# Attention and routed experts on one core: V gathers alone on SyncE's DMA queue, every other attention load and store on ScalarE's

## Chip, cores, metric
One NeuronCore of a Trainium2 chip runs the whole program in one launch. The metric is device time in microseconds (us), the median of several executions. A profiled execution gives the trace; all times inside the kernel below are counted from the start of its span.

## What is computed
Block-sparse attention (4 sequences, 8 heads, 768 tokens, head size 64, blocks of 32 tokens) and then a cosine router that sends each of the 3072 tokens to one of 8 experts (512 -> 1024 -> 512, ReLU), all in float32:

```python
mask = |blk_i - blk_j| <= 1, or either block is the first or the last, or blk_j in sampled_blocks[blk_i]
attn = softmax(where(mask, q @ k.T / 8, -1e9))          # per head
x = (attn @ v), heads side by side                      # (3072, 512)
idx = argmax(normalize(x) @ normalize(expert_emb).T);  gate = softmax(logits / tau)[idx]
out = gate * (relu(x @ w1[idx]) @ w2[idx])
```

## The kernel before
**Stages.** Attention runs in 24 steps `s` (and one closing step), six per sequence: `b, c = divmod(s, 6)`. A step handles a chunk of 128 query rows. The chunks are shifted by one block: chunk c = 0 of a sequence holds the two end blocks (first and last), whose rows attend to every key, and two inner blocks; the other chunks hold four inner blocks. Then come 25 expert tiles of 128 tokens (two of them mixed from two experts), which are bound by TensorE.

**Order.** In attention each engine runs its instructions in the order in which the Python code issues them; nothing is reordered. So does each of the two queues that issue plain DMAs: SyncE's (SP) and ScalarE's (ACT). A DMA issue stands in its engine's instruction stream, and an instruction that waits holds up everything behind it on that engine. The order of a step `s` on TensorE (PE) is: `score_near(s)` (scores against near and end blocks, tile `ac`), `score_far(s)` (against the three sampled blocks of each query block, tile `dps`), `weigh_near(s-1, 0)`, at c = 0 `score_ends` (`bps`, four head pairs), `turn_x(s-2)`, at c = 1 to 4 `turn_k` (transposes one head pair of the next sequence's K, tile `kps`), `weigh_far(s-1)` (probabilities times gathered V; at c = 1 also the end rows' part), `turn_q(s+1)` (transposes the next chunk's Q), `chunk_logits(s-2)`, `weigh_near(s-1, 1)`, `normalize(s-1)`. `ac`, `dps`, `bps` and `kps` take turns on two PSUM buffers (`big`), so every one of them waits until ScalarE or VectorE has read the one before last: the exponentials `pac` (of `ac`), `pd` (of `dps`) and `pb` (of `bps`), and the copy `kt` (of `kps`). `normalize` ends with a Square on ScalarE (tile `sq`), which stands on ScalarE just ahead of the next step's `pac`.

**Loads.** `load_q(s+2)` fetches a chunk of Q (256 KB, two buffers), `load_k` a head pair of K in two DMAs of 192 KB (two buffers), `load_v` the next sequence's V in ten DMAs (`vst`, `vg0`), `gather_v` the sampled V blocks: 12 DMAs of 64 KB a step (6 at c = 0), one for each query block and sampled slot, with three buffers `vg` in turn. Their addresses come from a table `offset` in SBUF, which the issuing engine reads into registers once for each c (`shifts`) and keeps. `gather_k` copies the sampled K blocks inside SBUF (GpSimd and VectorE), `near_v` near V blocks (GpSimd). `route` (line 771) stores each finished sequence's x rows to DRAM for the experts' gathers. Slots 0 and 1 of `gather_v`, all of `load_q` after the first two, `load_k`, most of `load_v`, the x stores and the expert weights (line 1060) are issued by SP; slot 2 of `gather_v` by ACT, in the middle of the step behind `pd`. SP's program at the start of step s is: `load_k`, `load_q(s+2)`, `gather_v(s+1)` slots 0 and 1, `load_v`.

**Start.** `load_block_ids`, four K pairs and two Q chunks, V of the first sequence, warm-up matmuls, constants, `build_choice` (the offset table and the bias that masks sampled blocks already covered), four `turn_k`, `turn_q(0)`, `gather_k(0)`, `gather_v(0)`, and the loop.

Of the kernel before, what the change touches and what calls it, by code (L numbers as in the profile page):

```python
# [20 lines left out]
P = 128  # L21
# [2 lines left out]
NB = S // BLK  # L24
NRAND = 3
NC = S // P
NPAIR = H // 2
N = B * S
NT = B * NC
# [100 lines left out]
def build_tokens(k, shifted):  # L130

    nc, pool = k.nc, k.const
    tok = pool.tile([P, NT], I32, name="tok")
    nc.gpsimd.iota(tok, pattern=[[-S, B], [-P, NC]], base=N + BLK * shifted, channel_multiplier=-1)
    if shifted:
        first = tok.rearrange("p (b c) -> p b c", c=NC)[:, :, 0]
        for rows, by in ((slice(0, BLK), -BLK), (slice(BLK, D), D - BLK - S)):
            nc.vector.tensor_scalar(out=first[rows], in0=first[rows], scalar1=by, scalar2=None, op0=ALU.add)
# [177 lines left out]
def pieces(c, shifted=True):  # L316

    if not shifted:
        return [(slice(0, P), c * P)]
    if c:  # L320
        return [(slice(0, P), c * P - BLK)]
    return [(slice(0, BLK), 0), (slice(BLK, D), S - BLK), (slice(D, P), BLK)]


def load_block_ids(k):
# [7 lines left out]
def build_choice(k):  # L333

    nc, pool = k.nc, k.setup
    r = pool.tile([P, NRAND, NI], F32, name="rand")
    nc.vector.tensor_copy(out=r, in_=k.idb[:, 1:NB - 1, :, 0].rearrange("p n r -> p r n"))
    at = pool.tile([P, NRAND, NI], F32, name="at_block")
    nc.vector.tensor_scalar(out=at, in0=r, scalar1=0.0, scalar2=float(NB - 1), op0=ALU.max, op1=ALU.min)
    k.offset = k.const.tile([P, NRAND, NI], I32, name="offset")  # L340
    nc.vector.tensor_scalar(out=k.offset, in0=at, scalar1=float(BLK), scalar2=None, op0=ALU.mult)
    own = pool.tile([P, NI], F32, name="own_block")
    nc.gpsimd.iota(own, pattern=[[1, NI]], base=1, channel_multiplier=0, allow_small_or_imprecise_dtypes=True)
    bad = pool.tile([P, NRAND, NI], F32, name="bad_block")
# [16 lines left out]
    k.shift = {}  # L361


def shifts(k, engine, s, c):

    blocks = [NG * c + g - 2 for g in blocks_of(c)]
    key = engine, s, c
    if key not in k.shift:
        _, values = k.nc.values_load_multi_w_load_instructions(
            k.offset[0:1, s, blocks[0]:blocks[-1] + 1], engines=(engine,), min_val=0, max_val=S - BLK,  # L370
            skip_runtime_bounds_check_because="the block numbers are clamped to the blocks there are")
        k.shift[key] = list(values)
    return k.shift[key]


def load_q(k, n, engine=None):

    b, c = divmod(n, NC)
    k.raw["q", n] = t = k.ld.tile([P, H, D], F32, name="qraw", tag="qraw", bufs=2)
    src = k.q[b].rearrange("h s d -> s h d")  # L380
    for rows, lo in pieces(c):
        (engine or k.nc.sync).dma_start(out=t[rows], in_=src[lo:lo + rows.stop - rows.start])


def load_k(k, g, pool=None):

    b, j = divmod(g, NPAIR)
    k.raw["k", g] = t = (pool or k.ld).tile([P, NC, 2, D], F32, name="kraw", tag="kraw", bufs=2)
    for h in range(2):
        k.nc.sync.dma_start(out=t[:, :, h], in_=k.k[b, 2 * j + h].rearrange("(c p) d -> p c d", p=P))  # L390


def load_v(k, b):
# [22 lines left out]
    return slice(lo, lo + BLK), tile // 2  # L416


def gather_v(k, n, slots):

    b, c = divmod(n, NC)
    k.vg[n] = t = k.vg_ring[n % len(k.vg_ring)]
    src = k.v[b].rearrange("h s d -> s h d")
    for s in slots:
        lanes = slice(s * BLK, (s + 1) * BLK)
        engine, queue = ((mybir.EngineType.SP, k.nc.sync) if s < 2 else (mybir.EngineType.Activation, k.nc.scalar))
        for g, shift in zip(blocks_of(c), shifts(k, engine, s, c)):
            queue.dma_start(out=t[lanes, g, :, 0:D], in_=src[bass.ds(shift, BLK)])


def near_v(k, n):
# [9 lines left out]
def turn_k(k, g):  # L441

    nc = k.nc
    b, j = divmod(g, NPAIR)
    raw = k.raw.pop(("k", g))
    ps = k.big.tile([P, 2, 512], F32, name="kps", tag="big")
    for c in range(NC):
        nc.tensor.transpose(ps[:, c // 3, c % 3 * P:(c % 3 + 1) * P], raw[:, c].rearrange("p h d -> p (h d)"), k.ident)  # L448
    copy = nc.scalar.copy if g % 2 else nc.vector.tensor_copy
    copy(out=k.kt[b % 2][:, j].rearrange("p (w t) -> p w t", w=2), in_=ps[:, :, 0:3 * P])  # L450
    if j == NPAIR - 1:
        nc.scalar.copy(out=k.ke[b % 2].rearrange("p j (n t) -> p j n t", n=2),
                       in_=k.kt[b % 2].rearrange("p j (n t) -> p j n t", t=BLK)[:, :, 0:NB:NB - 1])


def turn_q(k, n):
# [268 lines left out]
def route(k, b):  # L725
# [40 lines left out]
    with ExitStack() if k.attending else k.tc.issue_after(picked):  # L766
        nc.vector.reciprocal(out=x[:, :, :, P], in_=gate.broadcast_to([P, NC, ND]))
    yield
    for c in range(NC):
        for rows, lo in pieces(c, not k.exact):  # L770
            nc.sync.dma_start(out=k.x_dram[b * S + lo:b * S + lo + rows.stop - rows.start, :],
                              in_=x[rows, c].rearrange("p e w -> p (e w)"))
        yield

# [418 lines left out]
def attention_fast(n, ctx):  # L1193
# [27 lines left out]
    warm_up(n, 10)  # L1221
    for i in range(2):
        nc.gpsimd.memset(n.vst[i][:, :, :, D:D + 1], 1.0)
        nc.gpsimd.memset(n.vg0[i][D:P, :, D:D + 1], 1.0)
        nc.gpsimd.memset(n.qt_ring[i], 0.0)
    for vg in n.vg_ring:
        nc.gpsimd.memset(vg, 0.0)
# [13 lines left out]
    for s in range(NCH + 1):  # L1241
# [6 lines left out]
                if (when, part) == (s, half):  # L1248
                    what()

        if s == 0:
            for g in range(NPAIR, NPAIR + 2):
                load_k(n, g)
        if 2 <= c and b + 1 < B:
            g = NPAIR * (b + 1) + c
            if g < B * NPAIR:
                load_k(n, g)
        if s + 2 < NCH:
            load_q(n, s + 2)
        if s + 1 < NCH:  # L1260
            gather_v(n, s + 1, (0, 1))
        if 1 <= c <= NPAIR and b + 1 < B:
            for to, src in load_v(n, b + 1)[3 * c - 3:3 * c]:
                nc.sync.dma_start(out=to, in_=src)
        if s < NCH:
            score_near(n, s)
            score_far(n, s)
# [17 lines left out]
        if s >= 1:  # L1285
            weigh_far(n, s - 1)
        if s + 1 < NCH:
            gather_v(n, s + 1, (2,))
            near_v(n, s + 1)
            turn_q(n, s + 1)  # L1290
        if s >= 2:
# [236 lines left out]
```

## Time and profile before

| | |
|---|---|
| median of 3 runs | 687.17 us (683.32 to 691.76) |
| the profiled execution | 691.73 us, of which the span is 690.0 us |
| mean granted TensorE clock | 0.939 of full |
| busy: PE, PE weight loads, VectorE, ScalarE, GpSimd | 612.8, 479.5, 220.2, 120.6, 238.8 us |
| first score matmul of step 0 | 19.52 us |
| first matmul of the first expert tile | 312.76 us |
| SP's queue (q1) and ACT's queue (q10), bytes | 149.32 MB and 7.08 MB |

A row of the list of waits is: engine, line and tile that waited, whose end released it, us in total, times, longest. A row of the timeline is: start, length, engine (a `q` behind it means its instruction queue, where DMAs are issued), line, operation, out <- in, shapes, count; in brackets the idle time ahead and what ended it. A row of the chain is: start, length, what; it follows the end of the program back through whatever released each piece. The row of windows gives busy time (and count) of each engine, the granted clock, the share of time that the 16 DMA engines were busy, and GB/s.

### The profile page before, as it was taken

How to read it: one execution, taken by the hardware profiler on the slowest of the kernel's cores; microseconds unless marked ns; L12 is line 12 of the kernel's file. 1: busy time of each engine (PE TensorE's matmuls, PEld its weight loads, DVE VectorE, ACT ScalarE, POOL GpSimd, SP SyncE). 2: the span in 40 equal slices, each digit the busy share in tenths (PEclk: the TensorE clock that was granted, in tenths of full speed). 3: DMA queues.
4: the chain of work that ended last, by engine and by line, in shares of the span. 5: the costliest groups of instructions: out<-in, count | busy, mean ns of one | idle time of the engine just before them, and what ended most of it. 6: DMA issues, size and time to landing. Idle time of an engine off the chain costs nothing.

```text
span 690.0 us, 21717 instructions
## 1 busy us (share of the span) xinstructions
PE 612.8 (89%) x9016; PEld 479.5 (69%) x9016; DVE 220.2 (32%) x659; ACT 120.6 (17%) x274; POOL 238.8 (35%) x447
## 2 busy tenths in 40 slices
PE   5896679796979699578999999999999999999996
PEld 3795679686878689577677667766477664776673
DVE  4563225342354366323571111121211212112110
ACT  1532233243242253221000000000000000000000
POOL 5662314432442253500202224432244223442232
PEclk7899779897998799979899999999999999999999
DMA  9846645577557854789999999999899998999811
GB/s 189 162 100 145 138 108 122 124 149 170 148 114 156 173 137 107 193 190 301 394 368 402 376 356 322 336 339 345 313 361 409 392 406 320 372 410 392 317 47 31
DMA packets 192318, 171.32 MB, mean 248 GB/s; under 512 B 152712, under 2 KB 152840, under 8 KB 189394
## 3 DMA queue, kind: packets, MB, share of 16 engines
q1 hardware_dynamic: 157794, 149.32, 67.9%
q0 software_dynamic: 5216, 13.43, 5.4%
q10 hardware_dynamic: 29200, 7.08, 5.1%
q8 instruction: 73, 1.20, 0.7%
q14 instruction: 35, 0.29, 0.1%
HBM read 157.17 MB, written 12.90 MB: 246 GB/s over the span
## 4 chain that ended last, share of the span: by engine, by line
PE 82%; DMA 9%; SPq 3%; DVE 2%; issue 2%; ACT 1%; DVEq 0%; POOL 0%; ACTq 0%; POOLq 0%
PE hp L1107 24%; PE yp L1122 23%; PE av L572 10%; PE dps L537 6%; DMA qraw<-in_q_dram 3%; PE yp L679 3%; DMA vg<-in_v_dram 3%; PE ac L513 3%; PE xg_ps L461 2%; DMA kraw<-in_k_dram 2%; PE hp L1150 2%; PE yp L1170 2%; PE bps L559 2%; PE kps L448 2%; PE xg_ps L668 1%
## 5 line engine op out<-in xcount | busy, mean ns | idle before, releaser
L1107 PEld LDWEIGHTS hp<-xgt,w 128*128 128x128 f32 x1472 | 167.6, 192 | 10.2 <-issue 10.2
L1107 PE MATMUL hp<-xgt,w 128*128 128x128 f32 x1472 | 168.4, 275 | 0.0
L1122 PE MATMUL yp<-w,h 128*128 128x512 f32 x368 | 163.7, 598 | 0.0
L1122 PEld LDWEIGHTS yp<-w,h 128*128 128x128 f32 x368 | 69.0, 193 | 78.2 <-issue 77.5
L1031 POOL DMA_INDIRECT xg<-x_dram,quarter x88 | 88.5, 1006 | 30.1 <-issue 27.4
L478 POOL COPY kg<-kt 128x128 f32 x176 | 45.2, 299 | 101.6 <-issue 79.6
L1131 POOL DMA_INDIRECT out_dram<-y,slot_l x20 | 20.2, 1011 | 156.8 <-DVE y L1130 156.8
L1110 ACT ACTIVATE h<-hp 128x512 f32<-128x512 f32 x23 | 13.7, 597 | 294.0 <-PE hp L1107 267.2
L1114 DVE TENSOR_SCALAR h<-hp 128x512 f32<-128x512 f32 x23 | 15.9, 691 | 154.0 <-PE hp L1107 154.0
L465 DVE COPY qt<-xg_ps 64x512 f32<-64x512 f32 x48 | 33.1, 689 | 89.4 <-PE xg_ps L461 88.6
L438 POOL COPY vg<-vst 32x520 f32<-32x520 f32 x80 | 49.4, 617 | 34.1 <-PE av L572 24.7
L572 PE MATMUL av<-vst,pac 64*64 64x65 f32 x1056 | 49.3, 233 | 2.1 <-issue 1.4
L537 PE MATMUL dps<-qt,kg 128*64 128x64 f32 x1408 | 49.7, 230 | 0.9 <-issue 0.6
L537 PEld LDWEIGHTS dps<-qt,kg 128*64 128x64 f32 x1408 | 45.8, 143 | 3.2 <-issue 0.7
L461 PE MATMUL xg_ps<-ident,qraw 128*128 128x128 f32 x96 | 19.1, 333 | 29.1 <-DMA qraw<-in_q_dram 29.1
L572 PEld LDWEIGHTS av<-vst,pac 64*64 64x64 f32 x1056 | 41.5, 144 | 4.5 <-issue 2.3
L1130 DVE TENSOR_SCALAR y<-yp,gate 128x512 f32<-128x512 f32 x20 | 15.0, 751 | 82.3 <-PE yp L1122 70.2
L448 PE MATMUL kps<-ident,kraw 128*128 128x128 f32 x96 | 17.3, 333 | 21.9 <-DMA kraw<-in_k_dram 18.6
L542 ACT ACTIVATE pd<-dps,bias 128x256 f32<-128x256 f32 x88 | 34.7, 474 | 6.8 <-PE dps L537 6.4
L461 PEld LDWEIGHTS xg_ps<-ident,qraw 128*128 128x128 f32 x96 | 12.6, 166 | 31.6 <-issue 30.1
L513 PE MATMUL ac<-qt,ke 64*64 64x128 f32 (+1 forms) x384 | 30.5, 287 | 2.5 <-DVE qt L465 2.5
L572 PE MATMUL av<-vg,pd 128*32 128x65 f32 x1408 | 29.2, 235 | 3.0 <-DMA vg<-in_v_dram 1.9
(225 smaller groups left out, 661.8 us busy)
## 6 DMA issues: line engine op xcount, KB each, us to landing
w<-in_moe_w_dram SPq DMA_DIRECT2D x52, 2048.0 KB
vg<-in_v_dram SPq DMA_DIRECT2D x184, 64.0 KB
kraw<-in_k_dram SPq DMA_DIRECT2D x32, 192.0 KB
vg<-in_v_dram ACTq DMA_DIRECT2D x88, 64.0 KB
x_dram<-x SPq DMA_DIRECT2D x20, 258.0 KB
qraw<-in_q_dram SPq DMA_DIRECT2D x19, 256.0 KB
vst<-in_v_dram SPq DMA_DIRECT2D x18, 256.0 KB
w<-in_moe_w_dram SPq DMA_DIRECT2D x8, 512.0 KB
```

What stands on the lines that cost most here:

```text
L438: k.nc.gpsimd.tensor_copy(out=k.vg[n][NRAND * BLK:P, g], in_=k.vst[b % 2][rows, m])
L448: nc.tensor.transpose(ps[:, c // 3, c % 3 * P:(c % 3 + 1) * P], raw[:, c].rearrange("p h d -> p (h d)"), k.ident)
L461: k.nc.tensor.transpose(ps[:, j], raw[:, 2 * j:2 * j + 2, :].rearrange("p h d -> p (h d)"), k.ident)
L465: k.nc.vector.tensor_copy(out=t[rows, :, h], in_=ps[rows])
L478: copy(out=t[:, :, g, s * BLK:(s + 1) * BLK], in_=kt[:, :, bass.ds(shift, BLK)])
L513: nc.tensor.matmul(ps[D * r:D * (r + 1), h, lo:lo + cols.stop - cols.start], lhsT=keys, rhs=qt[rows, j, h, cols], start=True, stop=True)
L537: nc.tensor.matmul(out[D * r:D * (r + 1), NG * j + g], lhsT=kg[:, j, g, D * r:D * (r + 1)], rhs=qt[:, j, :, cols], start=True, stop=True)
L542: nc.scalar.activation(e[:, :, g].rearrange("p j h t -> p j (h t)"), out.rearrange("p (j g) h t -> p j g (h t)", g=NG)[:, :, g], ACT.Exp, ...
L572: k.nc.tensor.matmul(av[lanes, h // NPAIR, h % NPAIR * P:h % NPAIR * P + D + 1], lhsT=lhsT, rhs=rhs, start=first[0], stop=last, skip_group ...
L1031: k.nc.gpsimd.indirect_dma_start(out=x[:, g], out_offset=None, in_=quarters, in_offset=bass.IndirectOffsetOnAxis(ap=k.quarter[:, g, t:t + ...
L1107: nc.tensor.matmul(hp[:, f, :], lhsT=w1[:, d, (f0 + f) * P:(f0 + f + 1) * P], rhs=xt[:, d, :], start=(d == 0), stop=(d == ND - 1))
L1122: nc.tensor.matmul(yp, lhsT=h[:, f, :], rhs=w2[:, f, :], start=(f == 0), stop=(f == NF - 1))
```

## The change
- `gather_v` issues all three slots on SP. Slots 0 and 2 share one register: a fourth row of `offset` holds slot 2's offset times 1024 plus slot 0's, and each gather takes its part out by a mask or a shift.
- `load_q`, `load_v` inside the loop, `load_k` from the second sequence on and the x stores made during attention are issued by ACT. They move from the start of a step to its end, behind `normalize`: Q of chunk s+2 from the start of step s to the end of step s, V's parts from the start of steps 1 to 4 to the end of steps 0 to 3; the K pairs from the start of a step to the end of the one before.
- The first chunk of a sequence is laid out as last block, first block, then the two inner ones, so its rows are two runs in DRAM and no longer three.
- At the start SP issues all K and then all V of the first sequence, ACT only Q. VectorE clears the gather buffers in GpSimd's place; ScalarE runs one small Exp early; `turn_q(0)` comes first; for the first sequence `ke` (the end blocks' keys) is copied pair by pair and `score_ends` follows each pair, one pair behind `turn_k`; the bias is built behind them (`build_bias`).

```diff
+PACK = 1024
...
-    k.offset = k.const.tile([P, NRAND, NI], I32, name="offset")
-    nc.vector.tensor_scalar(out=k.offset, in0=at, scalar1=float(BLK), scalar2=None, op0=ALU.mult)
+    k.offset = k.const.tile([P, NRAND + 1, NB], I32, name="offset")
+    nc.vector.tensor_scalar(out=k.offset[:, 0:NRAND, 2:], in0=at, scalar1=float(BLK), scalar2=None, op0=ALU.mult)
+    nc.vector.tensor_scalar(out=at, in0=at, scalar1=float(BLK), scalar2=None, op0=ALU.mult)
+    nc.vector.scalar_tensor_tensor(out=k.offset[:, NRAND, 2:], in0=at[:, 2], scalar=float(PACK), in1=at[:, 0],
+                                   op0=ALU.mult, op1=ALU.add)
...
+def build_bias(k):      # the second half of build_choice
...
-        (engine or k.nc.sync).dma_start(out=t[rows], in_=src[lo:lo + rows.stop - rows.start])
+        k.nc.scalar.dma_start(out=t[rows], in_=src[lo:lo + rows.stop - rows.start])
...
+        engine = k.nc.scalar if b else k.nc.sync
+        engine.dma_start(out=t[:, :, h], in_=k.k[b, 2 * j + h].rearrange("(c p) d -> p c d", p=P))
...
-    for s in slots:
+    for s in range(NRAND):
         lanes = slice(s * BLK, (s + 1) * BLK)
-        engine, queue = ((mybir.EngineType.SP, k.nc.sync) if s < 2 else (mybir.EngineType.Activation, k.nc.scalar))
-        for g, shift in zip(blocks_of(c), shifts(k, engine, s, c)):
-            queue.dma_start(out=t[lanes, g, :, 0:D], in_=src[bass.ds(shift, BLK)])
+        for g, shift in zip(blocks_of(c), shifts(k, mybir.EngineType.SP, s if s == 1 else NRAND, c)):
+            if s == 0:
+                shift = shift & (PACK - 1)
+            elif s == 2:
+                shift = shift >> (PACK.bit_length() - 1)
+            if s != 1:
+                shift.max_val = S - BLK
+            k.nc.sync.dma_start(out=t[lanes, g, :, 0:D], in_=src[bass.ds(shift, BLK)])
...
+    queue = nc.scalar if k.attending else nc.sync        # in route: the x stores
...
     for g in range(NPAIR):
+        if g % 2 == 0:
+            load_q(n, g // 2)
         load_k(n, g, n.setup if g < 2 else None)
-        if g % 2 == 0:
-            load_q(n, g // 2, nc.scalar)
-    for i, (to, src) in enumerate(load_v(n, 0)):
-        (nc.sync if i % 2 else nc.scalar).dma_start(out=to, in_=src)
+    for to, src in load_v(n, 0):
+        nc.sync.dma_start(out=to, in_=src)
+    warm_up(n, 10)
+    for vg in n.vg_ring:
+        nc.vector.memset(vg, 0.0)
+    nc.scalar.activation(n.setup.tile([P, 1], F32, name="first_exp"), n.zeros[:, 0:1], ACT.Exp)
...
+    turn_q(n, 0)
     for g in range(NPAIR):
         turn_k(n, g)
-    turn_q(n, 0)
+        if g:
+            score_ends(n, 0, g - 1)
+    score_ends(n, 0, NPAIR - 1)
+    build_bias(n)
     gather_k(n, 0)
-    gather_v(n, 0, range(NRAND))
+    gather_v(n, 0)
...
     # top of step s: load_k, load_q(s + 2) and load_v are gone
-            gather_v(n, s + 1, (0, 1))
+            gather_v(n, s + 1)
...
-        ends = range(NPAIR) if c == 0 and s < NCH else ()
+        ends = range(NPAIR) if c == 0 and 0 < s < NCH else ()
...
     # behind weigh_near(s - 1, 1) and normalize(s - 1)
+        if s == 0:
+            for g in range(NPAIR, NPAIR + 2):
+                load_k(n, g)
+        if s + 2 < NCH:
+            load_q(n, s + 2)
+        if b + 1 < B:
+            g = NPAIR * (b + 1) + c + 1
+            if 1 <= c <= NPAIR and g < B * NPAIR:
+                load_k(n, g)
+            for to, src in load_v(n, b + 1)[3 * c:3 * c + 3]:
+                nc.scalar.dma_start(out=to, in_=src)
```

More of the change, by code (lines that the diff above doesn't have):

```diff
@@ L136, in build_tokens @@
         first = tok.rearrange("p (b c) -> p b c", c=NC)[:, :, 0]
-        for rows, by in ((slice(0, BLK), -BLK), (slice(BLK, D), D - BLK - S)):
-            nc.vector.tensor_scalar(out=first[rows], in0=first[rows], scalar1=by, scalar2=None, op0=ALU.add)
+        nc.vector.tensor_scalar(out=first[0:BLK], in0=first[0:BLK], scalar1=-S, scalar2=None, op0=ALU.add)
     part = pool.tile([P, 2, NT], I32, name="tok_part")
@@ L321, in pieces @@
         return [(slice(0, P), c * P - BLK)]
-    return [(slice(0, BLK), 0), (slice(BLK, D), S - BLK), (slice(D, P), BLK)]
+    return [(slice(0, BLK), S - BLK), (slice(BLK, P), 0)]
 def load_block_ids(k):
@@ L339, in build_choice @@
     nc.vector.tensor_scalar(out=at, in0=r, scalar1=0.0, scalar2=float(NB - 1), op0=ALU.max, op1=ALU.min)
-    k.offset = k.const.tile([P, NRAND, NI], I32, name="offset")
-    nc.vector.tensor_scalar(out=k.offset, in0=at, scalar1=float(BLK), scalar2=None, op0=ALU.mult)
+    k.offset = k.const.tile([P, NRAND + 1, NB], I32, name="offset")
[3 more added lines that the diff above has]
+                                   op0=ALU.mult, op1=ALU.add)
+    k.rand = r
+    k.shift = {}
+def build_bias(k):
+    nc, pool, r = k.nc, k.setup, k.rand
     own = pool.tile([P, NI], F32, name="own_block")
@@ L360, in build_choice @@
         nc.vector.tensor_scalar(out=k.bias[lanes], in0=bad[lanes, s], scalar1=NONE, scalar2=None, op0=ALU.mult)
-    k.shift = {}
 def shifts(k, engine, s, c):
-    blocks = [NG * c + g - 2 for g in blocks_of(c)]
+    blocks = blocks_of(c)
     key = engine, s, c
     if key not in k.shift:
+        most = (S - BLK) * (PACK + 1 if s == NRAND else 1)
         _, values = k.nc.values_load_multi_w_load_instructions(
-            k.offset[0:1, s, blocks[0]:blocks[-1] + 1], engines=(engine,), min_val=0, max_val=S - BLK,
+            k.offset[0:1, s, NG * c + blocks[0]:NG * c + blocks[-1] + 1], engines=(engine,), min_val=0, max_val=most,
             skip_runtime_bounds_check_because="the block numbers are clamped to the blocks there are")
@@ L373, in shifts, with load_q @@
     return k.shift[key]
-def load_q(k, n, engine=None):
+def load_q(k, n):
     b, c = divmod(n, NC)
@@ L389, in load_k @@
     for h in range(2):
-        k.nc.sync.dma_start(out=t[:, :, h], in_=k.k[b, 2 * j + h].rearrange("(c p) d -> p c d", p=P))
+        engine = k.nc.scalar if b else k.nc.sync
+        engine.dma_start(out=t[:, :, h], in_=k.k[b, 2 * j + h].rearrange("(c p) d -> p c d", p=P))
 def load_v(k, b):
@@ L416, in home, with gather_v @@
     return slice(lo, lo + BLK), tile // 2
-def gather_v(k, n, slots):
+def gather_v(k, n):
     b, c = divmod(n, NC)
@@ L450, in turn_k @@
     copy(out=k.kt[b % 2][:, j].rearrange("p (w t) -> p w t", w=2), in_=ps[:, :, 0:3 * P])
-    if j == NPAIR - 1:
-        nc.scalar.copy(out=k.ke[b % 2].rearrange("p j (n t) -> p j n t", n=2),
-                       in_=k.kt[b % 2].rearrange("p j (n t) -> p j n t", t=BLK)[:, :, 0:NB:NB - 1])
+    pairs = slice(j, j + 1) if b == 0 else slice(0, NPAIR)
+    if j == pairs.stop - 1:
+        nc.scalar.copy(out=k.ke[b % 2][:, pairs].rearrange("p j (n t) -> p j n t", n=2),
+                       in_=k.kt[b % 2][:, pairs].rearrange("p j (n t) -> p j n t", t=BLK)[:, :, 0:NB:NB - 1])
 def turn_q(k, n):
@@ L768, in route @@
     yield
+    queue = nc.scalar if k.attending else nc.sync
     for c in range(NC):
         for rows, lo in pieces(c, not k.exact):
-            nc.sync.dma_start(out=k.x_dram[b * S + lo:b * S + lo + rows.stop - rows.start, :],
+            queue.dma_start(out=k.x_dram[b * S + lo:b * S + lo + rows.stop - rows.start, :],
                               in_=x[rows, c].rearrange("p e w -> p (e w)"))
@@ L1214, in attention_fast @@
     for g in range(NPAIR):
+        if g % 2 == 0:
+            load_q(n, g // 2)
         load_k(n, g, n.setup if g < 2 else None)
-        if g % 2 == 0:
-            load_q(n, g // 2, nc.scalar)
-    for i, (to, src) in enumerate(load_v(n, 0)):
-        (nc.sync if i % 2 else nc.scalar).dma_start(out=to, in_=src)
+    for to, src in load_v(n, 0):
[4 more added lines that the diff above has]
+    nc.scalar.activation(n.setup.tile([P, 1], F32, name="first_exp"), n.zeros[:, 0:1], ACT.Exp)
     build_ident(n)
-    warm_up(n, 10)
     for i in range(2):
@@ L1226, in attention_fast @@
     for vg in n.vg_ring:
-        nc.gpsimd.memset(vg, 0.0)
         nc.gpsimd.memset(vg[:, :, :, D:D + 1], 1.0)
     build_choice(n)
+    turn_q(n, 0)
     for g in range(NPAIR):
         turn_k(n, g)
-    turn_q(n, 0)
+        if g:
+            score_ends(n, 0, g - 1)
+    score_ends(n, 0, NPAIR - 1)
+    build_bias(n)
     gather_k(n, 0)
-    gather_v(n, 0, range(NRAND))
+    gather_v(n, 0)
     near_v(n, 0)
@@ L1249, in planned @@
                     what()
[L1251 to L1259, printed above, removed]
         if s + 1 < NCH:
-            gather_v(n, s + 1, (0, 1))
-        if 1 <= c <= NPAIR and b + 1 < B:
-            for to, src in load_v(n, b + 1)[3 * c - 3:3 * c]:
-                nc.sync.dma_start(out=to, in_=src)
+            gather_v(n, s + 1)
         if s < NCH:
@@ L1287, in attention_fast @@
         if s + 1 < NCH:
-            gather_v(n, s + 1, (2,))
             near_v(n, s + 1)
```

## The prediction
> **What bounds the kernel now.** I read first the slices of the page, then who waited for whom on TensorE (PE) and SyncE (SP), then the chain and the timeline of single steps.
>
> ```profile
> PE   5896679796979699578999999999999999999996
> PEclk7899779897998799979899999999999999999999
> DMA  9846645577557854789999999999899998999811
> ```
>
> A slice is 17.25 us. From slice 18 on (310 us) PE is full: the 25 expert tiles, 378 us, which this change doesn't touch. In the 18 slices of attention PE has holes, the clock dips behind them, and the DMA engines are only about six tenths busy.
>
> ```profile
> PE xg_ps L461 <- DMA qraw<-in_q_dram: 29.1, 6, 7.7
> PE kps L448 <- DMA kraw<-in_k_dram: 18.6, 6, 5.2
> ...
> SPq L428 <- DMA vg<-in_v_dram: 66.1, 21, 9.2
> ```
>
> PE waits for Q and K, 29.1 and 18.6 us (3.7 of the latter at the start); nothing else there is over 3.4 us. SP waits 66.1 us ahead of V gathers, for other DMAs. One step in detail, first SP's queue, then PE:
>
> ```profile
> 66.16 0.95 SPq L382 DMA_DIRECT2D qraw<-in_q_dram  x1
> 68.24 8.89 SPq L428 DMA_DIRECT2D vg<-in_v_dram  x8
> 77.18 2.15 SPq L1264 DMA_DIRECT2D vst<-in_v_dram  x3
> 79.43 3.65 SPq L390 DMA_DIRECT2D kraw<-in_k_dram  x2
> 84.27 1.50 SPq L382 DMA_DIRECT2D qraw<-in_q_dram  x3
> ...
> 87.93 1.09 PE L461 MATMUL xg_ps<-ident,qraw 128*128 128x128 f32 x4 [7.32 <-DMA qraw<-in_q_dram]
> ```
>
> PE wants the Q that the program asks for 1.7 steps ahead, and SP issues it 3.7 us before use: SP lags by a whole step, because Q and K stand behind eight gathers. Those need no more than 4.02 us (the eight from 159.23) but took 8.89. In the trace each DMA raises one of eight semaphores, which both queues take in turn, and an issue first waits until the last DMA on its semaphore has landed. So SP's gathers wait for slot 2's, which ACT issues only behind its exponentials (72.67 in this step); a late K delays ACT's copy and with it those issues, and the lag feeds itself.
>
> The chain gives the price; `dps` starts 1.2 to 2.3 us into each step:
>
> ```profile
> 190.96 2.02 PE dps L537 x64
> ...
> 199.43 2.29 PE dps L537 x64
> ...
> 205.25 2.97 DMA kraw<-in_k_dram
> ...
> 215.92 2.02 PE dps L537 x64
> ...
> 224.30 2.02 PE dps L537 x64
> ...
> 229.25 5.63 DMA qraw<-in_q_dram
> ```
>
> Steps without a stall last 8.47 and 8.38 us here, the one with the late K 16.49. By the first `ac` matmul of each step in the timeline, ordinary steps without a stall take 8.0 to 8.8 (mean 8.4), c = 0 about 13, c = 1 about 11.7. Nine are longer: 11.1, 15.1, 16.7, 15.3, 16.8, 16.7, 15.6, 10.6, 18.1, together 135.9 instead of 75.6. The **excess is 60 us**, of which 44 are the waits after the start (29.1 + 18.6 - 3.7); 16 are slow matmuls behind them.
>
> **Removed: the lag, -60.** SP keeps the gathers alone. The quickest eights give 0.5 us each; a mask or shift for two in three adds at most 0.1 (a register operation in the gather's own rows has 46 ns), and the stray long issues (up to 1.45) about 0.8 a step: 7.5 us of an 8.4 us step. The gathers have three buffers, so this may run late by over a step before `weigh_far` notices. I cost SP at 0; if its slack is used up, each microsecond over 8.4 is paid in each step. ACT loses 88 issues of about 0.46 and gets 103 (28 Q, 24 K, 30 V, 21 stores), so its total hardly changes. Only the place does: ahead of `pac` instead of behind `pd`.
>
> One of the Trainium skill's rules speaks against any gain: "DMA: Bandwidth & Descriptors", section "Issuing engines are not separate DMA queues", says that all issuers share the same 16 engines, and that a second one saves only issue time. By it alone the stalls would stay and the sum would be 691.7. These rows weigh more with me:
>
> ```profile
> 118.00:130.00 12.00, 11.48 (x356) 10.62 (x351) 8.04 (x33) 7.39 (x17) 4.12 (x19) 1.00 0.34 75
> 153.00:166.00 13.00, 5.82 (x134) 5.61 (x136) 2.51 (x6) 0.23 (x2) 3.00 (x7) 0.71 0.90 181
> ```
>
> Before a stall the DMA engines are 0.34 busy (next to last number), in it 0.90: work is asked for late, then all at once. A sequence moves 10.6 MB (4.3 gathers, 1.6 each of Q, K, V and x); at 75/0.34 to 181/0.90, so 220 to 201 GB/s, that is 48 to 53 us against 58 of PE's steps without stalls (4 x 8.4 + 13 + 11.7). It fits, closely.
>
> **Added: ACT's issues ahead of `pac`.** `sq`, then `pac`, run 1.6 to 4 us into a step:
>
> ```profile
> 76.33 0.63 ACT L660 ACTIVATE sq<-x 128x512 f32<-128x512 f32 x1 [1.58 <-DVE x L655]
> 76.96 1.00 ACT L517 ACTIVATE pac<-ac 128x1024 f32<-128x1024 f32 x1
> ```
>
> Behind the new issues stand `pac` and `pd`; for `pac` waits the PSUM buffer of `kps` at c = 1 to 4 and of the first `bps` at c = 0. By quick rows an issue costs 0.45 (Q), 1.10 (a K pair), 0.45 to 0.72 (V part), 0.55 (store). Ahead of `pac`: 1.8 at c = 1, 3.0 at c = 2, 3.7 at c = 3, 2.0 at c = 4, 3.1 at c = 5, 1.5 at c = 0. In steps without a stall the slack between `pac`'s end and that matmul is 2.0, 0.8, 1.4, 1.6 and 0.1 (c = 5 has no `kps`). PE loses 0 + 2.2 + 2.3 + 0.4 + 0 + 1.4 = 6.3 a sequence, for three sequences 19. Then the semaphore waits: ACT's gathers show nearly none (four in 1.87 us), SP's 66.1/176 = 0.38 an issue; 57 issues in the losing steps make 0 to 21. I take 5, nearer to ACT's own rows: **+24** (10 to 40).
>
> **Q asked for a step later.** It is issued about 2.6 us into a step, and `turn_q` comes 6.2 to 6.9 in: 3.6 to 4.3 us. The chain's Q transfers took 2.66, 2.82, 5.24, 5.63 and 6.35. With 5.2, 1.2 is missing. At c = 0 and 1 `turn_q` comes after 9 us or more, and at c = 2 and 3 the `pac` wait covers it while K and V are loaded; ten steps remain: **+12** (0 to 38).
>
> Do stalls this short cost the clock? Behind gaps of 4.20 us and more the six `kps` took 1.51 us, behind one of 1.20 they took 0.84; in between no row decides. At 16/8 = 2 us each, nine 2.2 us stalls would add 18 at most; I take 0, nearer to 1.20. "TensorE: Matmul & The Clock Gate", section "HAM oscillation", of the Trainium skill sets the limit at gaps of some 3.4 us, which would make it 0 too.
>
> **The start.** Today K has landed at 12.39, but ACT is held in DMA issues until 12.80, loads its table until 14.1 and only then copies. Without that, `kps` goes on at 12.4 and `dps` can start near 16 instead of 21: -5. The 4.5 us of `bps` (23.1 to 27.6) move under K's arrival: -4.5. Against it: ACT issues eight DMAs (4.4) before the first ordinary `pac`, and K for step 1 is asked for later: +4.5. VectorE's three clears of 2080 columns cost 1.7 each (from 0.17 for 128 and 0.27 for 256), until 6.3, ahead of the table's arithmetic that begins at 5.06 today; K's arrival hides that, else it costs 1.3. The bias (9.98 to 12.85) now stands ahead of VectorE's K copies, also hidden until K is there, else up to 2.9. **-5** (-9.5 to +4).
>
> **The end.** Weights and gathers share SP's queue as today; the Q loads of the last steps meet them: **+2** (0 to 5).
>
> **Sum:** -60 - 5 + 24 + 12 + 2 = -27, so 691.7 becomes 664.7. That execution was 4.6 above the median of the runs; the median, 687.2, becomes **660**. Its own range is 640 to 676.
>
> **Rivals**, each on the median's scale.
> - Nothing hinders: loads land in time and ACT's issues vanish in slack: 687.2 - 65 + 10 = **632**. For it: DMA 0.34 busy before stalls, ACT a third busy. Against: slack of 0.8 and 0.1 us.
> - The stall changes place: Q comes too late every step. At 6.35, 2.4 are missing in 16 steps, 38; with 24 and 2 that is -65 + 64: **686**, no change. For it: the last two Q transfers were the slowest. Against: they met a backlog that should be gone.
> - ACT inherits SP's waits. Its issues are chained to the gathers' semaphores as SP's were to ACT's. SP's semaphore waits before its DMAs in attention sum to some 90 us; four steps in six can't cover them on ACT: 60, on top of 19 + 12 + 2 and lost -65: 687.2 + 28 = **715**, slower. It decides from about 3 us more per step in these steps. For it: exponentials, unlike gathers, have little slack. Against: ACT's gathers waited little.
> - The change doesn't do what it says where the split leaves SP lagging: 12 gathers at over 0.7 us would be the next bound, 8.4 a step; that ends near the second rival.
>
> **How the numbers follow.** Forecast 0.50, first rival 0.16, second 0.19, third 0.15. Within 2% (673.4 to 700.9; about what a measurement tells from no change) lie the second rival and a tenth of the forecast: 0.23; faster 0.62; slower 0.15. The range: all terms at their low ends give 628, all at their high ends 714; without these corners, and with half of the slower case, it is 632 to 704.
>
> **What would show it.** Right: PE's waits for Q and K together under 20 us, `kps` waiting for ACT `pac` at c = 2 and 3 by about 2 us, step lengths of 8.4 to 11, no 15s; SP's waits at gathers gone or harmless; the first expert matmul near 285; expert tiles unchanged. Wrong: Q waits in every step (second rival), long gaps in ACT's queue between its issues with PE waiting for ACT (third), or a first `dps` later than 18.

## Result, and the profile after

The changed kernel takes **717.39 us** (median of 4 runs, 713.25 to 719.66) against 686.92 for the kernel before: 1.043 times as long, interval 1.035 to 1.051. The forecast was 660. The profiled execution has a span of 717.9 us (before 690.0) and a mean granted clock of 0.912 (before 0.939). The first expert matmul comes at 343.1 instead of 312.6 us (its start in the timeline; the table above has 312.76, from the chain), and the experts then take 374.8 us instead of 377.4. So attention got 30 us longer, and nothing else did.

Section 2 of the page after the change, in slices of 17.9 us:

```profile
PE   7487789787896879985899999999999999999996
PEclk8876669979798879996889999999999999999999
DMA  9846544688436854459799999999989999899911
```

PE is full one slice later than before (19 instead of 18). In attention the DMA engines are still only about half busy, and the clock is lower.

What happened to PE is best split into idle time and slow time. The row of windows for attention alone (first `ac` to first expert matmul), before and after; the first pair of numbers behind the length is PE's busy time and matmuls, the third number from the end the granted clock:

```profile
19.52:312.60 293.08, 236.85 (x6827) 218.00 (x6827) 126.59 (x423) 100.05 (x238) 110.96 (x301) 0.89 0.64 143
```

```profile
20.05:343.11 323.06, 257.81 (x6644) 235.64 (x6640) 123.42 (x417) 97.77 (x235) 110.13 (x299) 0.83 0.61 132
```

PE does the same matmuls (the trace after lacks 2.7% of the records). It is idle for 65.2 us instead of 56.2, **9 us more**, and busy for 257.8 instead of 236.9, **21 us more**, because the granted clock fell from 0.89 to 0.83. The clock has two values in the records, 1.0 and 0.5, so it stood at half for about (1 - 0.83) x 2 x 323 = 110 us and before for 64.

PE's waits after the change (line numbers are those of the changed kernel: 464 is `kps`, 589 `av`, 478 the Q transposes):

```profile
PE kps L464 <- ACT pac L534: 21.1, 7, 4.9
PE av L589 <- DMA vg<-in_v_dram: 19.9, 9, 7.5
PE yp L230 <- DVE emb L224: 7.4, 1, 7.4
...
PE xg_ps L478 <- DMA qraw<-in_q_dram: 3.3, 3, 2.6
```

Before, Q and K made PE wait for 29.1 and 18.6 us; now Q takes 3.3 and K 0.8. In their place stand `pac` (21.1) and gathered V (19.9, before 1.9). Where the gathers were late, the list of SP's waits tells:

```profile
SPq L444 <- DMA qraw<-in_q_dram: 76.3, 17, 7.7
SPq L444 <- DMA kraw<-in_k_dram: 33.4, 12, 9.2
```

SP issues almost nothing but gathers in attention, yet they wait 110 us for Q and K to land. No gather uses Q or K. What a gather waits for is a semaphore: in the trace's records SP and ACT take the same eight in turn (numbers 100, 102, 103 and 105 to 109), and an issue waits until the DMA that last had its semaphore has landed. ACT is held the same way. Its timeline in step 2:

```profile
47.15 0.39 ACTq L392 DMA_DIRECT2D qraw<-in_q_dram  x1
...
48.22 0.56 ACTq L401 DMA_DIRECT2D kraw<-in_k_dram  x1
...
50.31 1.35 ACTq L1319 DMA_DIRECT2D vst<-in_v_dram  x2
51.77 1.02 ACT L534 ACTIVATE pac<-ac 128x1024 f32<-128x1024 f32 x1 [3.91 <-DMA kraw<-in_k_dram]
```

The two `vst` have the semaphores of that Q and of the first of the two K, so ACT waits for what it has itself just issued, and `pac` stands behind it: it starts 3.9 us behind `sq` (the bracket), where issues of 3.0 were reckoned at c = 2; one step later it is 5.5, where 3.7 were. The chain shows the loop that comes of it, from one step's normalization to the next:

```profile
60.82 0.70 DVE x L672
...
62.14 0.19 ACT sq L677
62.33 0.39 ACTq L401
...
62.76 4.00 DMA kraw<-in_k_dram
...
66.77 4.48 DMA vg<-in_v_dram
...
71.30 2.16 PE av L589 x60
...
78.00 0.70 DVE x L672
...
78.84 3.24 DMA qraw<-in_q_dram
...
82.10 4.93 DMA vg<-in_v_dram
...
87.17 2.55 PE av L589 x64
```

Normalize, then ACT issues K; K lands, and that lets SP issue a gather (the K of 62.76 and the gather of 66.77 have the same semaphore, 102); the gather lands, and that lets PE weigh far, and so reach the next normalize. From 60.82 to 78.00, a lap is **17.2 us**, where an undisturbed step takes 8.4. Three buffers for gathered V do not help, because a step has twelve gathers and the semaphores let SP run at most eight DMAs ahead of ACT.

By place the 30.5 us are: 4.9 before step 2 begins (44.68 instead of 39.76), 15.3 in the fifteen ordinary steps, 1.3 at c = 0 and 1, and 9.0 in the last step with its closing one.

### The profile page after: what moved, and what is told of

It reads as the page before. It is cut to its first block, busy times and chain, and to the rows that moved or that the text cites. A ratio compares the mean times of both kernels' runs of the same rounds, so it can differ in the third digit from the quotient of the medians.

```text
span 717.9 us, 21825 instructions
## 1 busy us (share of the span) xinstructions
PE 636.9 (89%) x9016; PEld 500.4 (70%) x9016; DVE 222.5 (31%) x663; ACT 121.4 (17%) x278; POOL 233.3 (33%) x444
## 4 chain that ended last, share of the span: by engine, by line
PE 73%; DMA 13%; DVE 4%; issue 4%; ACT 2%; SPq 2%; ACTq 1%; POOL 1%; POOLq 0%; DVEq 0%
PE hp L1125 23%; PE yp L1140 22%; PE av L589 11%; DMA vg<-in_v_dram 4%; PE yp L696 4%; DMA kraw<-in_k_dram 4%; DMA qraw<-in_q_dram 3%; PE xg_ps L478 3%; PE hp L1168 2%; PE yp L1188 2%; DVE x L672 2%; DMA x_dram<-x 1%; PE bps L576 1%; PE kps L464 1%; PE dps L554 1%
## 5 line engine op out<-in xcount | busy, mean ns | idle before, releaser
L589 PE MATMUL av<-vg,pd 128*32 128x65 f32 x1408 | 39.4, 266 | 28.3 <-DMA vg<-in_v_dram 19.9
L1128 ACT ACTIVATE h<-hp 128x512 f32<-128x512 f32 x23 | 13.7, 597 | 291.5 <-PE hp L1125 291.5
L589 PEld LDWEIGHTS av<-vg,pd 128*32 128x32 f32 x1408 | 32.6, 137 | 35.0 <-issue 13.0
L589 PE MATMUL av<-vst,pac 64*64 64x65 f32 x1056 | 51.7, 243 | 1.0 <-issue 0.7
L589 PEld LDWEIGHTS av<-vst,pac 64*64 64x64 f32 x1056 | 43.9, 153 | 3.8 <-issue 1.4
L464 PE MATMUL kps<-ident,kraw 128*128 128x128 f32 x96 | 17.8, 335 | 22.2 <-ACT pac L534 21.1
L530 PE MATMUL ac<-qt,ke 64*64 64x128 f32 (+1 forms) x384 | 33.8, 311 | 1.6 <-ACT pd L559 0.9
L696 PEld LDWEIGHTS yp<-en,xt 128*128 128x128 f32 x192 | 32.8, 257 | 2.1 <-ACT sq L677 1.2
```

The source lines that it names most:

```text
L530: nc.tensor.matmul(ps[D * r:D * (r + 1), h, lo:lo + cols.stop - cols.start], lhsT=keys, rhs=qt[rows, j, h, cols], start=True, stop=True)
L589: k.nc.tensor.matmul(av[lanes, h // NPAIR, h % NPAIR * P:h % NPAIR * P + D + 1], lhsT=lhsT, rhs=rhs, start=first[0], stop=last, skip_group ...
L696: k.nc.tensor.matmul(ps[:, 0:E], lhsT=xt[:, j], rhs=k.en[:, j, :], start=(j == 0), stop=(j == ND - 1))
```

## Experiments

Ratios are to the kernel before, run in the same job on the same chip (686.4 to 688.4 us).

**All loads on SP's queue, in the new places.** Is it the split, or the new places and the new start?

```diff
-        k.nc.scalar.dma_start(...)            # load_q; load_k, load_v in the loop and x stores likewise
+        (k.nc.scalar if n < 2 else k.nc.sync).dma_start(...)
```

> The changed kernel with the loop's Q, K and V loads and the x stores issued by SP instead of ACT, at the same places in the program; the start is unchanged. Theory A (the two queues are chained by the eight semaphores that they take in turn: a gather on SP can be at most eight DMAs ahead of ACT's loads, which stand behind the Square of each step, and ACT's later loads wait for its own earlier ones to land): with one queue the chain across queues is gone, PE's waits for vg (19.9 us) and for pac (21.1 us) fall below 5 us together, steps come down from about 15 to 9 to 10 us, the time to 650 to 680. Rival B (the gathers are late because SP and the DMA engines have no more to give, and Q and K are asked for too late): only the pac waits go, Q and K waits come in their place since they now stand behind gathers; 695 to 720.

686.59 us, ratio 0.997 (0.994 to 1.001), between the ranges of the two theories. The waits for `pac` and gathered V are gone, as theory A had it; Q takes their place, as B had it:

```profile
PE xg_ps L478 <- DMA qraw<-in_q_dram: 29.6, 10, 4.0
PE kps L464 <- DMA kraw<-in_k_dram: 7.8, 2, 7.0
```

SP's timeline shows twelve gathers in a row, first after the change (the end of one step's gathers and the start of the next's), then here (one step's):

```profile
54.24 17.89 SPq L444 DMA_DIRECT2D vg<-in_v_dram  x12
```

```profile
68.22 8.92 SPq L444 DMA_DIRECT2D vg<-in_v_dram  x12
```

Half the time, with more work on the queue. The row shown is among the longer ones here: a step's twelve took 7.1 to 10.7 us (median 8.3), after the change 8.0 to 25.1 (median 13.2). One queue carries all the loads 31 us faster than two, so the split is the cause of the loss. What is left here is SP's own issuing: its gathers wait no more than 5.2 us for other DMAs, but a step's gathers alone take about as long as an undisturbed step (8.4), and Q stands behind them.

**The old start with the new loop.** How much does the start cost?

```diff
-    for to, src in load_v(n, 0): nc.sync.dma_start(out=to, in_=src)   # and the rest of the new start
+    for i, (to, src) in enumerate(load_v(n, 0)): (nc.sync if i % 2 else nc.scalar).dma_start(out=to, in_=src)
...
+    build_bias(n)
     for g in range(NPAIR): turn_k(n, g)
     turn_q(n, 0)
```

> The changed kernel with the start as before: loads of V on both queues, GpSimd clears the gather buffers, no early Exp, turn_q(0) behind turn_k, end scores and bias as before; the loop as changed. In the changed kernel step 2 began at 44.7 us, before at 39.8. If the new start costs what this shows, the time falls by about 5 us, to 712 (theory A and B alike); if step 1's 20.7 us come from the loop's new loads at the end of step 0 and not from the start itself, step 2 begins at 44 or later and the time stays at 717 or rises to 722.

708.86 us, ratio 1.028 (1.021 to 1.035): 8.5 better, but not at the start. Step 2 begins at 46.69, 2.0 later than with the new start; the gain comes later in the loop (the first expert matmul at 338.2 instead of 343.1). That is neither of the two outcomes expected. So the new start in itself saves a little, and the gain is made elsewhere. Another start also shifts which DMA shares a semaphore with which; whether that is the reason was not tested.

**The same loads issued by GpSimd.** GpSimd's DMAs use other semaphores (114 to 121 in the trace), so the tie is cut while the places stay.

```diff
-        k.nc.scalar.dma_start(...)            # the same four places as above
+        (k.nc.scalar if n < 2 else k.nc.gpsimd).dma_start(...)
```

> The changed kernel with the loop's Q, K and V loads and the x stores issued by GpSimd, whose DMAs take another set of semaphores; same places in the program. Theory A: SP's gathers run ahead by their three buffers, PE's waits for vg and pac both fall below 5 us, steps of 8.5 to 10 us where GpSimd (5 of 12 us busy, plus about 5 issues of some 1 us, the mean of its indirect DMAs) keeps up; 655 to 685. Rival B (DMA engines and SP at their limit): vg waits stay near 20 us, only the pac waits go; about 695. If GpSimd becomes the bound, the wait list shows PE or VectorE waiting for kg and vg copies; then 690 to 720 without vg waits on DMAs.

682.11 us, ratio 0.989 (0.982 to 0.996): 35 us better than the changed kernel. The first rows of PE's waits:

```profile
PE av L589 <- issue: 18.6, 11, 3.5
PE yp L230 <- DVE emb L224: 6.8, 1, 6.8
```

`kps` no longer waits for `pac`, and nothing waits for gathered V: now SP's gathers wait mostly for their buffers (47.3 us behind `av`), as they should. New are gaps inside groups of matmuls that nothing in the profile releases ("issue", 18.6 us, after the change 5.3).

**ACT's loads behind `pd`.** Does it help to take only `pac` out of the way? (V's parts also come one step later here.)

```diff
             weigh_far(n, s - 1)
+        # load_q, load_k and load_v stand here, behind this step's exponentials
         if s + 1 < NCH:
             near_v(n, s + 1)
...
-        # and not behind normalize
```

> The changed kernel with the loop's loads moved from the end of the step to behind weigh_far, so that on ACT they stand behind pd and no longer ahead of pac (V's ten parts one step later, at c = 1 to 4, as before). Theory A: the pac waits (21.1 us) go, the chain between the queues stays, now through pd instead of the Square: vg waits of 10 us or more stay; 685 to 705. Rival C (the loss is only ACT's issues ahead of pac, and what follows from them): vg waits go too, steps of 8.5 to 10; 655 to 680.

715.05 us, ratio 1.039 (1.030 to 1.047): no gain, and outside both ranges. The wait moved, so the sign was theory A's and the price was not:

```profile
PE av L589 <- DMA vg<-in_v_dram: 51.3, 16, 8.0
```

The wait of `kps` for `pac` is down from 21.1 to 0.8, but ACT's loads are issued later, so SP's gathers get their semaphores later. Of the two halves of the tie, taking away the one on ACT only feeds the other.

**A third of the gathers left out.** This version does not fetch sampled slot 2.

```diff
-    for s in range(NRAND):
+    for s in range(2):
```

> The changed kernel without the gathers of sampled slot 2 (that slot's V rows stay zero): 8 gathers a step on SP instead of 12, ACT's loads and everything else unchanged; read by its attention stage, since the routing changes. Theory A (a gather can be no more than eight DMAs ahead of ACT's loads): the eight gathers of a step now fit between two sets of ACT's loads, so PE's waits for vg fall from 19.9 us below 6; the pac waits (21.1 us) stay, since ACT's later loads still wait for its own earlier ones; attention ends 20 to 30 us earlier, near 310. Rival B (gathers late for lack of DMA rate): a quarter of the gathers less is a tenth of all bytes; vg waits fall by a third, attention ends 10 us earlier.

Its total, 707.69 us, says little, because tokens then go to other experts and the experts take longer (408 us). The first expert matmul comes at 295.2 us, 48 earlier, more than either theory had. The wait for gathered V vanishes altogether, which fits theory A: eight gathers a step fit into eight semaphores. But a third of SP's issues is gone too, so this run alone doesn't tell the two apart. What stays is PE's wait for `pac` (18.2 us).

**One queue, in the old places, slot 2 on SP.**

```diff
-            queue.dma_start(...)              # kernel before: slot 2 on ACT, behind pd
+            k.nc.sync.dma_start(...)          # all three slots on SP, offsets packed as in the change
```

> The kernel before with slot 2's gathers on SP too (packed offsets, the two-run layout of the first chunk): one queue for everything but the first loads, loads ahead of the gathers at the top of the step, the start as before. One queue with loads at the end of a step gave 686.6, with 29.6 us of Q waits; in it twelve gathers took 8.6 to 8.9 us and the loads 2 to 5, more than PE's 8.4 us a step. Theory A with that bound: Q and K waits fall to about 15 us since they are asked for a step earlier, the rest is SP's issue time (17 issues of 0.6 to 0.7 us, 10.5 to 12 us a step): 665 to 685. If the asking place did not matter, 678 (686.6 less the 8.5 of the start).

679.33 us, ratio 0.987 (0.980 to 0.994). Taking slot 2's gathers (four a step, two at c = 0) off ACT gains 7 us, with the packed offsets and the new layout of the first chunk as the only other changes: before, SP waited 66.1 us ahead of gathers for other DMAs; now the largest such row is 2.9 us, though SP has half as many gathers again to issue. PE's waits for Q and K still sum to 34.2 us, where about 15 were expected.

**GpSimd for all loads, and GpSimd for the patient ones only.** Both have the old start and the old places; the edit is shown against the version just above.

```diff
-            k.nc.sync.dma_start(...)          # load_q, load_k, load_v, x stores
+            k.nc.gpsimd.dma_start(...)        # first version: all four; second: only load_v and x stores
```

> Gathers alone on SP; Q, K and V loads and x stores on GpSimd, at the top of the step as before and not at its end; the start as before. With these loads on GpSimd at the end of the step the time was 682.1, with the new start's loss of 8.5 in it. Theory A: 682 less 8.5 less most of the 6.8 us of Q waits: 665 to 675. GpSimd as the bound: its issues (0.8 to 1.4 us each) now stand ahead of gather_k's copies; PE waits for kg, 680 to 700.

> All gathers, Q and K on SP at the top of the step; only V's loads and the x stores (3 a step, none urgent) on GpSimd; the start as before. SP then has 14 issues a step, 8.5 to 10 us, against PE's 8.4 to 13. Theory A with SP's issue time as the bound: Q and K waits under 12 us, 650 to 670, the fastest of these. If SP's issue time is not the bound of the one queue, it is no faster than the one-queue kernel with early loads, within 1%.

The first gives 684.32 us (0.995, 0.991 to 0.998), with "issue" gaps of 14.6 us on `av`, and lies above the 665 to 675 expected. The second gives **670.74 us, ratio 0.974 (0.967 to 0.980)**, faster than both kernels. SP keeps gathers, Q and K, all of them urgent; V and x have a sequence's time.

**The second version with V and x on ACT.** Only the issuer of 51 DMAs in the whole of attention differs, 30 parts of V and 21 stores.

```diff
-                nc.gpsimd.dma_start(out=to, in_=src)      # load_v; the x stores likewise
+                nc.scalar.dma_start(out=to, in_=src)
```

> The same kernel (670.7) with V's loads and the x stores issued by ACT instead of GpSimd, at the same places: only the issuer differs, 3 DMAs a step. Theory A (ACT's and SP's DMAs share eight semaphores, GpSimd's do not): SP's gathers, Q and K wait for ACT's DMAs again and ACT's for SP's; SP's waits for vst and x_dram come up, 683 to 705. If the place on ACT ahead of pac is the cost and the semaphores are not: 1.7 us ahead of pac in four steps of six, partly covered by the slack, 672 to 680, without waits of SP for vst or x_dram.

711.89 us, ratio 1.034 (1.028 to 1.041): **41 us slower**, with the same transfers and places, and more than the 683 to 705 expected. SP's waits within attention (44 to 312 us of the trace):

```profile
SPq L444 <- DMA vst<-in_v_dram: 37.3, 13, 9.2
...
SPq L444 <- DMA x_dram<-x: 18.4, 6, 4.9
...
SPq L401 <- DMA vst<-in_v_dram: 11.9, 4, 5.2
```

In the faster version none of the three rows exists. A gather waits for a V part of the next sequence and for a store of finished rows, neither of which it has anything to do with. PE pays for it mostly at K:

```profile
PE kps L464 <- DMA kraw<-in_k_dram: 33.5, 7, 7.7
PE av L589 <- DMA vg<-in_v_dram: 9.6, 6, 2.7
```

The rival, that the place on ACT ahead of `pac` is the cost, fails: `kps` waits only 1.4 us for `pac` here. Nothing but the issuer changed, and the waits that appeared name its DMAs. This settles the cause: ACT's DMAs and SP's are one chain, and GpSimd's are not part of it.

**The start on top of the faster version**, first whole, then only its order of scores.

```diff
+    turn_q(n, 0)
     for g in range(NPAIR):
         turn_k(n, g)
-    turn_q(n, 0)
+        if g:
+            score_ends(n, 0, g - 1)
+    score_ends(n, 0, NPAIR - 1)
+    build_bias(n)
...
```

> The kernel with V and x on GpSimd (670.7) with the whole new start: all K ahead of all V on SP, VectorE clears the gather buffers, early Exp, turn_q(0) first, end scores pair by pair, bias behind them. In the loop as changed, step 2 began at 44.7 with the new start and at 46.7 with the old one, though the whole was 8.5 us slower with the new one. If the start is worth what its own steps show, step 2 begins 2 us or more earlier than the 43.8 of the old start here, and the time falls to 664 to 669. If it costs the 8.5 us, 679.

> The same kernel (670.7) with turn_q(0) first, the end scores pair by pair and the bias behind them; loads, clears and the rest of the start as before. Step 0 loses its 4.5 us of end scores, but the transposes of later K pairs now stand behind the scores of earlier ones. If they hide under K's arrival: 666 to 668. If they only move ahead of the first scores (in the changed kernel the first score matmul came at 20.05, no earlier than before): within 1 us of 670.7.

668.77 us (0.971, 0.964 to 0.978) and 668.26 us (0.971, 0.964 to 0.977): 2 to 2.5 better than without, within the intervals of both. Step 2 begins at 39.74 instead of 43.79 in the second, so 4 us are won at the start, and most of them are given back later: the first expert matmul comes at 289.0 instead of 289.5. Where ACT's and SP's loads are not chained, the new start does no harm.

**Filling PE's gaps.** The rows of windows say that most of the loss is slow matmuls. Do the waits make the clock low, though each is short?

```diff
-    for j in range(ND):
+    for j in [i for i in range(ND) for _ in range(4)]:      # turn_x: each transpose four times
         k.nc.tensor.transpose(ps[:, j], k.x[b][:, c, j, 0:P], k.ident)
```

> The changed kernel with each transpose of turn_x issued four times in a row: 12 more transposes a step, 2.0 us of useless TensorE work (from 0.66 us for four), placed ahead of the point where PE then waits for pac or for gathered V. In the trace of the changed kernel attention is 30 us longer than before: PE idle 53.3 us instead of 43.9 in gaps over 1 us, and PE busy 257.8 us instead of 236.9, with the granted clock at half for 109 us instead of 65, in 13 stretches that each begin behind a gap of 1.8 to 7.5 us. Theory that the gaps cause the half clock, and that its threshold lies near 2.2 us: most gaps of 2.7 to 3.9 us shrink to 0.7 to 1.9, half-clock time falls under 70 us; the useless work costs nothing in the steps with a stall and 2 us in each of some ten others, and the matmuls at full clock give back some 15 to 20: 705 to 725 us, though 44 us of work were added. Rival, that the clock is low for another reason (the loads' traffic, a limit on power) or that the lower clock cost nothing because the chain of DMAs sets the step: half-clock time stays at 95 us or more, and the time is 735 or more.

721.09 us, ratio 1.048 (1.041 to 1.055). Attention alone:

```profile
20.33:343.40 323.07, 272.07 (x6921) 251.12 (x6917) 125.25 (x418) 97.89 (x235) 110.13 (x298) 0.89 0.60 134
```

Attention takes as long as without the filling (323.07 and 323.06), though 23 steps have 2 us more of matmuls. The clock rose from 0.83 to 0.89, and its records for attention sum to 68 us at half speed instead of 109, so PE's busy time grew by 14 us and not by 46. So the gaps do cause the low clock; both numbers lie within the range expected. But 14 us more of busy PE time did not lengthen attention, nor did the higher clock shorten it. So PE's busy time alone does not set the length; that fits a pace set by the loop of loads, in which PE's slow matmuls are only a part. What the low clock by itself cost the changed kernel, no run here isolates.

## Why the prediction was wrong, point by point

- **"Removed: the lag, -60" failed**, at the words "I cost SP at 0". The prediction had read from the trace that both queues share eight semaphores and that SP was late because of ACT. But it took the change to untie them, because SP's list held only gathers and those have three buffers. The tie works by the order of DMAs over both queues, not by what a queue carries. The change ties *twelve* gathers to up to six loads that stand behind each step's normalize on ACT, and SP's gathers wait 110 us for those. PE's waits for Q, K, gathered V and, ahead of `kps`, `pac` sum to 49.6 us before and 45.1 after: of the 60 hardly 5 were gained, and a wait of 7.4 for `emb` was added. The Trainium skill ("DMA: Bandwidth & Descriptors", section "Issuing engines are not separate DMA queues") says that a second issuing engine saves only issue time. The runs agree that it buys no more than that (686.59 us with one queue for the same loads and places, 717.39 with two), and show that it can cost: 670.74 against 711.89 us for the choice of issuer alone.
- **"Do stalls this short cost the clock? I take 0" failed too.** The stalls became more and shorter: nine gaps of PE over 1 us before, mean 4.9, fourteen after, mean 3.8. Thirteen of the fourteen brought a stretch at half clock of 3.4 to 13.7 us; the one that did not lasted 1.36. In PE's own account the clock's share is the 21 us of busy time that were added, near the bound of 18 that the prediction gave and then put at nothing; how much of it lengthened attention is not shown (see the filled gaps). The stalls were also longer than the 2.2 us reckoned: at `kps` 3.0 in the mean.
- **ACT's issues ahead of `pac`, +24 (10 to 40)**: measured 21.1 at `kps` and 2.5 at `bps`, together 23.6. The size was right, the makeup was not, so the agreement is partly luck. At c = 2 and 3 of the first three sequences (six steps) ACT's issues between `sq` and `pac` took 2.3 to 3.6 us, where 3.0 and 3.7 were reckoned. Its waits between them took 0.6 to 3.4, together 11 us, where the prediction took 5 for all steps.
- **Q asked for a step later, +12 (0 to 38)**: 3.3, since steps of 14 to 17 us leave Q time. With one queue the same places cost 29.6, but there Q also stands behind a step's gathers, so the term by itself was not measured.
- **The start, -5 (-9.5 to +4)**: step 0 lasted 3.9 instead of 9.6 us, so moving `bps` under K's arrival worked, -5.7. But the first `dps` came at 21.25 and not near 16 (the end scores now stand in PE's queue between the K transposes), no earlier than before, and step 1 lasted 20.7 instead of 10.65: the router's `emb` stood on SP behind chained gathers and held PE 7.4 us, and some 6 us at half clock followed. In sum +4.9.
- **The end, +2 (0 to 5)**: +9.0. Here the chain of the profile runs from a store of x on ACT (6.8 us until it has landed) to a gather on SP and on to PE, so it is the same tie.
- **The third rival** ("ACT inherits SP's waits", 715 us) had the sign, the size and the place of the tie. It held ACT to be the one that waits; SP waited more (110 us), and PE paid about equally at `pac` and at V, so that its 715 fell so near is partly luck. Its evidence against, that ACT's gathers waited little, came from issues that stood late in the step, after the waiting had been done by SP.

## What to carry to other kernels

Before a load is moved to another queue, find what an *issue* waits for, not only what the data waits for: here two in-order queues that share eight completion semaphores are one chain, and every transfer is held by the slowest neighbour within eight DMAs, however many buffers it has. Keep urgent loads together on one queue, and give patient ones an issuer outside the chain: here the issuer of 51 DMAs made 41 us. When a stall is traded for several shorter ones, count the clock for each.

## What the hardware showed

- **Here gaps from 2.24 us on nearly always halved the clock.** In step 2 after the change, PE's timeline and then the windows of the gap and of what follows:

```profile
52.85 1.54 PE L464 MATMUL kps<-ident,kraw 128*128 128x128 f32 x6 [2.69 <-ACT pac L534]
```

```profile
50.16:52.85 2.69, 0.00 (x1) 0.01 (x1) 0.69 (x1) 1.08 (x2) 0.37 (x2) 0.87 0.97 175
52.85:62.00 9.15, 9.15 (x164) 8.50 (x164) 2.93 (x10) 2.76 (x7) 2.47 (x4) 0.50 0.42 92
```

  A gap of 2.69 us, and then 9.15 us in which PE is busy throughout at a clock of 0.50. Over the attention of thirteen profiled executions (all but that of the whole new start), 92 of 93 gaps of 2.24 us or more that began at full clock had a stretch at half clock (3.4 to 17 us, in multiples of 3.41) begin within them or in the 3.41 us behind them; of 66 gaps from 1.0 to 1.75 us, 15 had; in between, 20 of 30. The Trainium skill ("TensorE: Matmul & The Clock Gate", section "HAM oscillation") gives some 3.4 us as the limit. Here the measured one is lower. The prediction's stalls of 2.2 us lay just where most gaps already cost the clock, and its 0 leaned on the wrong side.
- **A gather's issue costs more than its quickest rows.** With all loads on SP's queue a step's twelve took 7.1 to 10.7 us, median 8.3 or 0.69 each, where the prediction had put 7.5 with its allowance for long issues and 0.5 for the quickest; in a step of 8.4 that leaves SP no room for its other loads.
- **DMAs issued by GpSimd come with holes in PE's groups.** The row `av` behind "issue" has 3.2 us before, 5.3 after the change and at most 6.1 in the other versions without such DMAs, but 7.6 and 10.0 in two with V and x on GpSimd, and 14.6 and 18.6 with all loads there. What makes them was not found.
